# Sliding-window attention with sinks and a squared-ReLU layer on one core: eight sinks per head, and two head pairs to a tile of sinks

## The chip, the cores and the metric

The kernel runs on one core of a Trainium2 chip. The metric is the time of one execution on the device in microseconds (us). The engines are named as in the profile: PE (TensorE, matmuls and transposes), PEld (its weight loads), DVE (VectorE), ACT (ScalarE), POOL (GpSimd) and SP (SyncE, which issues the DMAs).

## The reference, cut to what matters

Attention over 4 batches, 8 heads, 768 positions and a head dimension of 64, in which a query sees the first `n_sink` (4) keys, the sinks, and its own window of the last `window` (128) keys. Then a two-layer network over the 3072 tokens with 512 inputs and 2048 hidden units, with g = s * relu(h)^2 + b between the layers.

```python
keep = is_sink | in_window                    # pos < n_sink, 0 <= rel < window
scores = np.where(keep, scale * q @ k.T, -1e9)
a = np.exp(scores - scores.max(-1, keepdims=True))
a = a / (a.sum(-1, keepdims=True) + 1e-9)
x = (a @ v)                                   # transposed to (B*S, H*D)
r = np.maximum(x @ w_in, 0.0)
out = (s * (r * r) + b) @ w_out
```

## The kernel before

The tokens are cut into 8 chunks of 384 (half a sequence of one batch, in the order `ORDER`), each of 3 blocks of 128 queries. The expert layer of chunk c ("block c" of the run) is interleaved with the attention of chunk c+1, so there are a lone attention chunk at the start, seven mixed blocks, and a lone expert layer at the end. Float32 matmuls run in a rounded form, so an operand is split in a rounded part and its remainder, and two or three matmuls are added.

The expert layer is a list of 32 steps (`moe_steps`): `l1(f)` (12 matmuls of 384 columns, line 598, then ReLU on ACT into the tile `r`, line 601, the square on DVE, line 603, and the split of g on ACT and DVE, lines 605 and 606), and `l2(f)` (9 matmuls of 512 columns, line 617). Their order is l1(0), l1(1), l1(2), l2(0), l1(3), l2(1), ..., l1(15), l2(13), l2(14), l2(15): from step 2 on l1(f) is step 2f - 2, and l2(f) is step 2f + 3. At the last l2 the three output tiles are copied out of PSUM into tiles of the tag `ot` and stored.

Chunks 0 and 1 take another way to attention (`Plain`). Chunks 2 to 7 take `attn_slots`: 24 units (8 heads by 3 query blocks) in a pipeline over slots t. In slot t stand `unit_a` of unit t, `unit_b` of unit t - 4 and `unit_c` of unit t - 7, and at its end the transpose of unit t - 3 (`turn`, line 324).

- `unit_a`: two score matmuls (lines 303 and 304) over the keys of the window and `NS` sinks, 272 columns (144 for the first query block of a sequence), masked minimum on DVE (308), exponential on ACT with the row sums into `zz` (314), addition of the two half windows on POOL (317), and a copy of the sinks' weights, three times, into the tile `psk` of the pair of heads (318).
- `unit_b`: the transposed weights are masked and split into `hl` (337 to 340). After the last unit of a pair 1/sum is made and written, split in two, into columns 96 to 99 of `psk`.
- `unit_c`: the matmuls with the values (368, 376). After the last unit of a head the result goes to the tile `y` (383, 384); after the last of a pair, three 128x128 transposes turn `psk` (390), and the result is copied to `xsk` (392, with a remainder on DVE, 393).
- `sinks` (line 399: one matmul with the sinks' values `vs`, added to y) and `scaled` (line 406: one matmul with the selector `sel`, which spreads 1/sum, multiplied into y), then the split into `k.x`, which the next l1 reads. `load_sinks` fetches `vs` through a staging tile of the tag `ot`.

`ahead` and `ends` in `attn_slots` give the slots of loads, preparation, `sinks` and `scaled` of each pair: loads 2 or 5 slots before the pair's first unit; `sinks` and `scaled` 3 and 4 slots behind the pair's transposes, 2 and 2 for the last pair. Now the transposes of a chunk's four pairs stand in slots 12, 18, 24 and 30.

The loop at lines 771 to 783 gives slots to steps: slot i is issued behind step floor(30 i / 33), so slots 0 and 1, 11 and 12, 22 and 23 share one. This program order is a priority for a planner, which then orders each engine's queue by its own cost model: an instruction that it takes to be ready can go ahead of one that stands before it. TensorE's queue in the trace follows the program order but for a few places.

Tiles of a tag share `bufs` buffers; a tile waits until the tile before it in its buffer has been read for the last time. `psA` has 5 PSUM banks for h, scores, o, ts, os and zb. `r` has 2 buffers (`RB`), `y` 2, `xsk` 1.

Of the kernel before, what the change touches and what calls it, by code (L numbers as in the profile page):

```python
# [6 lines left out]
F32 = mybir.dt.float32  # L7
# [8 lines left out]
P = 128  # L16
B, H, S, D = 4, 8, 768, 64
ORDER = ((0, 0), (1, 0), (0, 1), (1, 1), (2, 0), (2, 1), (3, 0), (3, 1))
NS = 16
BLK = 3  # L20
# [12 lines left out]
NARROW, NEARLY = 2, 8  # L33
RB, VB = 2, 2
E0 = 8
FN, FB, FC = (4, 2), (6, 6), (9, 10)
LB, LC, LD, LDL, L2 = 4, 7, (3, 4), (2, 2), 2


@with_exitstack  # L40
def tile_kernel(ctx, tc, qT, kT, k0, v, vsk, n_sink, window, w, s, b, out):
# [14 lines left out]
    late = []  # L56
    m_all = const.tile([P, 6 * P], MDT, tag="m", name="m_all")
    m_full = [m_all[:, a * P:(a + j + 1) * P] for j, a in ((0, 0), (1, 1), (2, 3))]
# [8 lines left out]
    split = const.tile([P, 2, P], U8, tag="split", name="split")  # L67
    msk = const.tile([P, 3 * W + P + NS], MDT, tag="msk", name="msk")
    m_1, m_odd, m_even = (msk[:, j * W:(j + 1) * W] for j in range(3))
    m_0 = msk[:, 3 * W:]  # L70

# [61 lines left out]
    def constants2():  # L133

        spread = wk.tile([P, P], F32, tag="y", name="spread", bufs=2)
        nc.gpsimd.memset(spread, 0.0)
        for j in range(2):
            nc.gpsimd.affine_select(
                out=spread[96:P].rearrange("p (a d) -> p a d", a=2), in_=spread[96:P].rearrange("p (a d) -> p a d", a=2),
                pattern=[[1, 2], [0, D]], compare_op=ALU.not_equal, fill=1.0, base=2 * j, channel_multiplier=-1)  # L140
# [12 lines left out]
        mask(m_even[:, P:P + NS], snk[:, :NS])  # L153
        cp = nc.gpsimd.tensor_copy
        upm, lom = m_full[2][:, P:2 * P], m_full[2][:, 2 * P:]
        cp(out=m_0[:, NS:], in_=lom)
        for m, l0 in ((m_1, P), (m_even, P + NS), (m_odd, P)):
            cp(out=m[:, :P], in_=upm)
            cp(out=m[:, l0:l0 + P], in_=lom)
        cp(out=m_odd[:, 2 * P:], in_=m_even[:, P:P + NS])  # L160

# [11 lines left out]
    def load_weight(f):  # L173
        if f + 1 < NF:
            raw = place(f + 1).bitcast(I32).rearrange("p c t f -> p c (t f)")
            nc.sync.dma_start(raw, w[f])
            raws[f] = [raw[:, c].rearrange("p (f t) -> p f t", t=2) for c in range(2)]
            if f + 1 < NF - NARROW:
                raws[f] = [raw.rearrange("p c (f t) -> p c f t", t=2)]
        else:  # L180
            raws[f] = []
            for j, tag in enumerate(("vv", "vv", "y", "y")):
                raw = wk.tile([P, DM // 2, 2], I32, tag=tag, name="wraw", bufs=2)
                nc.sync.dma_start(raw.rearrange("p f t -> p (f t)"), w[f, :, j // 2, j % 2 * DM:(j % 2 + 1) * DM])
                raws[f].append(raw)
# [53 lines left out]
    def load_pair(k, pr):  # L239

        pp = Chunk()
        k.pairs[pr] = pp
        half = k.half
        nkb, k0, kw, v0 = 3 + half, (0, 288)[half], (416, 544)[half], half * 2
        pp.q = wk.tile([P, CH], F32, name="qraw", tag="qraw", bufs=1)
        nc.sync.dma_start(pp.q, qT[k.b, pr, :, half * CH:(half + 1) * CH])
        pp.v = wk.tile([P, 4, 2, D], F32, name="vraw", tag="vraw", bufs=1)
        nc.sync.dma_start(pp.v[:, :nkb], v[k.b, pr, :, v0:v0 + nkb])
        for hh in range(2):
            hd = Chunk()  # L250
# [22 lines left out]
    def prep_head(k, h):  # L273
# [18 lines left out]
    def unit_a(k, h, i, sc):  # L292
# [33 lines left out]
    def unit_b(k, h, i, tp):  # L326
# [17 lines left out]
        pp = k.pairs[h // 2]  # L344
        if h % 2 == 1 and i == BLK - 1:
            zr = wk.tile([P, 2, BLK, 2], F32, tag="zr", name="zr")
# [4 lines left out]
            nc.gpsimd.tensor_copy(out=pp.psk[:, :, 96:98], in_=zh.bitcast(F32))  # L351
            nc.vector.tensor_tensor(out=pp.psk[:, :, 98:100], in0=zr[:, 1], in1=zh.bitcast(F32), op=ALU.subtract)

    def unit_c(k, h, i):
# [24 lines left out]
        if i == BLK - 1:  # L379
            a, c = (0, D) if h % 2 == 0 else (D, 0)  # L380
            if h % 2 == 0:
                pp.x = wk.tile([P, CH + P], F32, tag="y", name="y", bufs=2)
            nc.scalar.copy(pp.x[a:a + D], hd.o[c:c + D])
            nc.vector.tensor_tensor(out=pp.x[a:a + D], in0=hd.o[a:a + D], in1=pp.x[a:a + D], op=ALU.add)
            if h % 2 == 1:
                nc.gpsimd.tensor_tensor(out=pp.x[:, CH - P:CH], in0=pp.x[:, CH - P:CH], in1=pp.x[:, CH:], op=ALU.add)
                pp.x = pp.x[:, :CH]
                ts = ps("ts")
                for j in range(BLK):
                    nc.tensor.transpose(ts[:, j * P:(j + 1) * P], pp.psk[:, j, :], ident)  # L390
                pp.xs = wk.tile([P, CH], F32R, tag="xsk", name="xsk", bufs=1)
                nc.scalar.copy(pp.xs, ts[:, :CH])
# [194 lines left out]
    def moe_steps(x, store, wk, before=None, last=False):  # L587
# [3 lines left out]
        def l1(f):  # L591
# [242 lines left out]
```

## Time and profile before

| | |
|---|---|
| median of 3 runs | 736.4 us (736.2 to 736.9) |
| profiled execution, its own time | 739.3 us |
| span of that execution | 737.2 us |
| mean granted clock of TensorE | 0.977 |

An excerpt of the page: the span in 40 equal slices of 18.4 us. Each digit is the busy share of a slice in tenths; PEclk is the clock that TensorE was granted.

```profile
PE   6788899899999999999999999999999999999996
...
DVE  6779999738984788757785588847886589743331
ACT  5978888568774787656884677746775677633222
POOL 2254555348991689616773589816775389710000
PEclk9879989999999999999999999999999999999998
```

A matmul's end is modelled and overlaps the next one's start, so prices of matmuls are read from start to start.

### The profile page before, as it was taken

What the parts mean: (1) busy time and instruction counts of PE and PEld (TensorE: products, weight loads), DVE (VectorE), ACT (ScalarE), POOL (GpSimd) and SP (SyncE); (2) the same over time, 40 slices, a digit from 0 to 9 for tenths busy, and PEclk for the clock granted to TensorE, in tenths of its full rate; (3) what the DMA queues carried; (4) which work ended last, traced back from release to release, by engine and by line L of the source; (5) the groups of instructions that cost most, each with busy time, mean ns of one, the idle gap of its engine ahead of it and who ended that gap; (6) DMA issues with size and microseconds to landing.
All of it is one profiled execution on the core that took longest, in us unless ns stands there. A gap on an engine that the chain in (4) does not pass through costs nothing.

```text
span 737.2 us, 11878 instructions
## 1 busy us (share of the span) xinstructions
PE 704.9 (96%) x3848; PEld 622.0 (84%) x3848; DVE 516.1 (70%) x1213; ACT 480.0 (65%) x1169; POOL 396.3 (54%) x641
## 2 busy tenths in 40 slices
PE   6788899899999999999999999999999999999996
PEld 3367677789988999999998999999999999989895
DVE  6779999738984788757785588847886589743331
ACT  5978888568774787656884677746775677633222
POOL 2254555348991689616773589816775389710000
PEclk9879989999999999999999999999999999999998
DMA  7844122041210212111121222111111212000001
GB/s 280 337 171 193 33 102 72 15 139 51 80 63 31 84 55 65 34 61 54 46 64 44 82 63 64 46 54 49 56 53 45 84 42 59 12 18 26 1 1 47
DMA packets 27221, 53.01 MB, mean 72 GB/s; under 512 B 3472, under 2 KB 15376, under 8 KB 25232
## 3 DMA queue, kind: packets, MB, share of 16 engines
q1 hardware_dynamic: 27152, 52.18, 21.2%
q8 instruction: 32, 0.52, 0.3%
q14 instruction: 37, 0.30, 0.1%
HBM read 45.88 MB, written 6.29 MB: 71 GB/s over the span
## 4 chain that ended last, share of the span: by engine, by line
PE 79%; DVE 10%; DMA 3%; ACT 3%; POOL 2%; issue 1%; SPq 1%; POOLq 0%; ACTq 0%; DVEq 0%
PE po L617 32%; PE h L598 32%; PE o L376 3%; PE sc L303 2%; PE sc L304 2%; PE sc L324 2%; DMA vf<-in_v 2%; DMA w<-in_w 2%; DVE w L214 2%; DVE g L606 1%; DVE wt L213 1%; PE ts L390 1%; POOL w L216 1%; DVE smf L528 1%; DVE r L603 1%
## 5 line engine op out<-in xcount | busy, mean ns | idle before, releaser
L598 PE MATMUL h<-x,w 128*128 128x384 f32 x1536 | 299.8, 344 | 1.1 <-ACT tf L542 0.8
L617 PE MATMUL po<-w,g 128*128 128x512 f32 x1152 | 298.0, 404 | 0.0
L598 PEld LDWEIGHTS h<-x,w 128*128 128x128 f32 x1536 | 268.6, 189 | 6.7 <-ACT tf L542 1.1
L617 PEld LDWEIGHTS po<-w,g 128*128 128x128 f32 x1152 | 212.4, 191 | 45.0 <-issue 2.7
L603 DVE SCALAR_TENSOR_TENSOR r<-h,sb,r 128x384 f32<-128x384 f32 x128 | 78.6, 614 | 82.5 <-ACT r L601 82.2
L606 DVE SCALAR_TENSOR_TENSOR g<-r,sb,g 128x384 fp32r<-128x384 f32 x128 | 102.0, 797 | 39.0 <-ACT g L605 38.2
L340 POOL TENSOR_TENSOR hl<-two,hl 128x256 fp32r<-128x256 f32 x128 | 99.3, 776 | 21.4 <-ACT hl L339 18.2
L601 ACT ACTIVATE r<-h 128x384 f32<-128x384 f32 x128 | 62.3, 487 | 66.7 <-PE h L598 66.5
L605 ACT ACTIVATE g<-r,sb 128x384 fp32r<-128x384 f32 x128 | 78.7, 615 | 34.1 <-DVE r L603 32.8
L317 POOL TENSOR_TENSOR sm<-sm 128x128 f32<-128x128 f32 x128 | 68.0, 531 | 59.5 <-ACT sm L314 55.5
L314 ACT ACTIVATE sm<-sm,negm 128x272 f32<-128x272 f32 (+1 forms) x144 | 73.1, 507 | 35.4 <-DVE negm L308 31.0
L308 DVE CUSTOM_DVE_ANT_0 sm<-sc,msk 128x272 f32<-128x272 f32 (+1 forms) x144 | 60.4, 419 | 40.4 <-PE sc L304 32.6
L284 POOL TENSOR_TENSOR kl<-kraw,kh 128x544 fp32r<-128x544 f32 (+1 forms) x48 | 63.1, 1315 | 21.7 <-ACT kh L282 21.7
L339 ACT CAST hl<-two 128x256 fp32r<-128x256 f32 x128 | 50.6, 395 | 31.6 <-DVE two L337 31.6
L216 POOL TENSOR_TENSOR w<-w 128x1024 int32<-128x1024 int32 (+1 forms) x17 | 32.6, 1919 | 45.6 <-DVE w L214 25.1
L337 DVE TENSOR_TENSOR two<-sc,split 128x256 f32<-128x256 f32 x128 | 53.0, 417 | 4.4 <-POOL hl L340 4.2
L318 POOL COPY psk<-sm 128x48 f32<-128x48 f32 x144 | 40.7, 282 | 26.7 <-ACT sm L314 26.1
L289 POOL TENSOR_TENSOR vv<-vraw,vv 128x256 fp32r<-128x256 f32 (+1 forms) x48 | 34.4, 718 | 24.6 <-ACT vv L288 24.6
L376 PE MATMUL o<-hl,vv 128*128 128x256 f32 (+1 forms) x256 | 44.5, 276 | 0.0
L303 PE MATMUL sc<-kh,qs 128*128 128x272 f32 (+1 forms) x144 | 42.6, 298 | 0.0
L376 PEld LDWEIGHTS o<-hl,vv 128*128 128x128 f32 x256 | 39.6, 189 | 2.9
L304 PE MATMUL sc<-kl,qs 128*128 128x272 f32 (+1 forms) x144 | 41.3, 288 | 0.0
(129 smaller groups left out, 904.4 us busy)
## 6 DMA issues: line engine op xcount, KB each, us to landing
w<-in_w SPq DMA_DIRECT2D x15, 1024.0 KB, 9.0
kraw<-in_kT SPq DMA_DIRECT2D x32, 272.0 KB, 2.6
out<-ot SPq DMA_DIRECT2D x24, 256.0 KB, 2.0
qraw<-in_qT SPq DMA_DIRECT2D x24, 192.0 KB, 2.4
vraw<-in_v SPq DMA_DIRECT2D x16, 256.0 KB, 2.7
kraw<-in_kT SPq DMA_DIRECT2D x16, 208.0 KB, 2.4
vsraw<-in_vsk SPq DMA_DIRECT2D x24, 64.0 KB, 2.0
vraw<-in_v SPq DMA_DIRECT2D x8, 192.0 KB, 2.4
```

Of the source, the lines that this page charges most:

```text
L284: nc.gpsimd.tensor_tensor(out=hd.kl[:, :kw], in0=hd.k[:, :kw], in1=hd.kh[:, :kw].bitcast(F32), op=ALU.subtract)
L308: nc.vector.tensor_tensor_reduce(out=sm[:, :n], in0=sc[:, :n], in1=m, scale=-0.125, scalar=BIG, op0=ALU.add, op1=ALU.min, accum_out=negm[: ...
L314: nc.scalar.activation(sm[:, :n], sm[:, :n], AF.Exp, bias=negm[:, uu], scale=-1.0, accum_out=pp.zz[:, i, hh:hh + 1])
L317: nc.gpsimd.tensor_tensor(out=sm[:, c1:c1 + P], in0=sm[:, p1:p1 + P], in1=sm[:, c1:c1 + P], op=ALU.add)
L340: nc.gpsimd.tensor_tensor(out=lo, in0=both, in1=hi.bitcast(F32), op=ALU.subtract)
L376: nc.tensor.matmul(hd.o[:, q0:q0 + n * P], hd.vv[:, kb, :], hd.hl[:, t, c0 * P:(c0 + n) * P], start=(hd.n == 0), stop=(i == BLK - 1 and kb ...
L598: nc.tensor.matmul(h[:, :CH], weight[f][:, 0, wi, cc * P:(cc + 1) * P], x[xi][:, cc, :], start=(i == 0), stop=(i == 11))
L601: nc.scalar.activation(r, h[:, :CH], AF.Relu, scale=1.0 / WUP)
L603: nc.vector.scalar_tensor_tensor(out=r, in0=h[:, :CH], scalar=sw_ap, in1=r, op0=ALU.mult, op1=ALU.mult)
L605: nc.scalar.activation(gg[:, 0, :], r, AF.Identity, bias=b_ap, scale=1.0)
L606: nc.vector.scalar_tensor_tensor(out=gg[:, 1, :], in0=r, scalar=b_ap, in1=gg[:, 0, :].bitcast(F32), op0=ALU.add, op1=ALU.subtract)
L617: nc.tensor.matmul(po[tb], gg[:, gi, tsl], weight[f][:, 1, wi, :], start=(f == 0 and i == 0), stop=(f == NF - 1 and i == 2))
```

## The change

The number of sinks that the fast way holds per head goes from 16 to 8. Three copies of four heads' sinks then fill 96 rows of a `psk` tile as three copies of two heads' did, and rows 96 to 103 hold 1/sum of two pairs, so two pairs of heads share one `psk` tile, its three transposes and one `xsk`. The transposes stand behind the last unit of every second pair (slots 18 and 30), `sinks` and `scaled` follow 3 and 4, then 6 and 7 slots later, and 2, 2, 3, 3 for the last two pairs; `sel` gets a second half, `load_sinks` moves to 11 slots behind the pair's first unit, and a chunk has 34 slots instead of 33. `y` gets a third buffer and `r` loses one; in block 0 odd f take the buffer of `xsk` for it. One mask moves into another tile. For blocks 1 to 7 a list takes the place of the even spreading: slot t goes behind step t minus the number of entries of `TWOS` not over t, so slots 3/4, 12/13, 15/16, 27/28 and 30/31 share a step, and the last slot, 33, stands behind step 28.

```diff
-NS = 16
+NS = 8
-RB, VB = 2, 2
+RB, VB = 1, 2
+TWOS = (4, 13, 16, 28, 31)
-LB, LC, LD, LDL, L2 = 4, 7, (3, 4), (2, 2), 2
+LB, LC, LD, LDL, L2 = 4, 7, ((3, 4), (6, 7)), ((2, 2), (3, 3)), 2
...
-    m_1, m_odd, m_even = (msk[:, j * W:(j + 1) * W] for j in range(3))
-    m_0 = msk[:, 3 * W:]
+    m_1, m_even = (msk[:, j * W:(j + 1) * W] for j in range(2))
+    m_odd, m_0 = m_all[:, 4 * P:], msk[:, 2 * W:]
...
-    sel = const.tile([P, P], F32R, tag="sel", name="sel")
+    sel = const.tile([P, 2, P], F32R, tag="sel", name="sel")
...
-        for j in range(2):
-            nc.gpsimd.affine_select(
...
+        for j in range(4):
+            row = spread[96:P, j // 2].rearrange("p (a d) -> p a d", a=2)
+            nc.gpsimd.affine_select(out=row, in_=row, pattern=[[1, 2], [0, D]], compare_op=ALU.not_equal, fill=1.0,
+                                    base=2 * j, channel_multiplier=-1)
...
+        mask(m_odd[:, 2 * P:], snk[:, :NS])
...
-        for m, l0 in ((m_1, P), (m_even, P + NS), (m_odd, P)):
+        for m, l0 in ((m_1, P), (m_even, P + NS)):
...
-        cp(out=m_odd[:, 2 * P:], in_=m_even[:, P:P + NS])
...
-        pp.psk = psks[(k.c * (H // 2) + pr) % 2]
+        pp.psk = psks[(k.c * (H // 4) + pr // 2) % 2]
...
-        nc.gpsimd.tensor_copy(out=pp.psk[:, i, :6 * NS].rearrange("p (t x) -> p t x", t=3)[:, :, hh * NS:(hh + 1) * NS],
+        nc.gpsimd.tensor_copy(out=pp.psk[:, i, :12 * NS].rearrange("p (t x) -> p t x", t=3)[:, :, h % 4 * NS:(h % 4 + 1) * NS],
...
+            if h % 4 == 3:
                 ts = ps("ts")
                 for j in range(BLK):
                     nc.tensor.transpose(ts[:, j * P:(j + 1) * P], pp.psk[:, j, :], ident)
-                pp.xs = wk.tile([P, CH], F32R, tag="xsk", name="xsk", bufs=1)
+                pp.xs = k.pairs[h // 2 - 1].xs = wk.tile([P, CH], F32R, tag="xsk", name="xsk", bufs=1)
...
-        nc.tensor.matmul(zb[:, :CH], sel, pp.xs, start=True, stop=True)
+        nc.tensor.matmul(zb[:, :CH], sel[:, pr % 2], pp.xs, start=True, stop=True)
...
-            todo = ((-5, load_pair, pr), (-5, load_keys, h), (-2, load_sinks, pr), (-2, prep_head, h), (-2, load_keys, h + 1),
+            todo = ((-5, load_pair, pr), (-5, load_keys, h), (11, load_sinks, pr), (-2, prep_head, h), (-2, load_keys, h + 1),
...
-            t = 2 * BLK * (pr + 1) - 1 + LC
-            for d, fn in zip(LD if pr < H // 2 - 1 else LDL, (sinks, scaled)):
+            t = 4 * BLK * (pr // 2 + 1) - 1 + LC
+            for d, fn in zip((LD if pr < H // 2 - 2 else LDL)[pr % 2], (sinks, scaled)):
...
-            r = wk.tile([P, CH], F32, tag="r", name="r", bufs=RB)
+            r = wk.tile([P, CH], F32, tag="xsk" if before and f % 2 else "r", name="r", bufs=RB)
...
+    step_of = [t - sum(t >= b for b in TWOS) for t in range(4 * BLK * 2 + LC + LDL[1][1])]
...
-            while i < len(slots) and i * (len(steps) - 2 * (c > 0)) < (j + 1) * len(slots):
+            while i < len(slots) and (step_of[i] <= j if c else i * len(steps) < (j + 1) * len(slots)):
```

## Rows read from the trace of the kernel before

**Rows 1.** The page's first part: each engine's busy us, share of the span, instructions.

```profile
PE 704.9 (96%) x3848; PEld 622.0 (84%) x3848; DVE 516.1 (70%) x1213; ACT 480.0 (65%) x1169; POOL 396.3 (54%) x641
```

**Rows 2.** Stretches: length in us, each engine's busy us, granted clock, DMA share.

```profile
0.00:61.00 61.00, 46.98 (x234) 29.62 (x235) 45.89 (x146) 44.83 (x101) 21.08 (x29) 0.86 0.68 260
61.00:153.00 92.00, 81.25 (x412) 64.57 (x411) 79.49 (x139) 67.46 (x131) 44.39 (x28) 0.93 0.22 77
238.70:324.45 85.75, 85.67 (x486) 78.73 (x485) 63.78 (x149) 59.08 (x151) 59.30 (x103) 1.00 0.19 57
324.45:407.74 83.29, 83.29 (x469) 76.52 (x469) 59.37 (x149) 56.30 (x151) 47.90 (x87) 1.00 0.18 57
```

**Rows 3.** TensorE's waits from 153 to 731 us: total, times, longest.

```profile
PE h L598 <- DVE xsk L393: 0.3, 1, 0.3
```

**Rows 4.** TensorE's waits from 0 to 153 us, the two largest groups.

```profile
PE o L551 <- ACT tf L542: 7.5, 5, 2.4
PE tp L540 <- DVE smf L528: 7.4, 3, 2.9
```

**Rows 5.** Groups by form, TensorE, whole span: the transposes of line 390.

```profile
L390 PE MATMUL ts<-identr,psk 128*128 128x128 f32 x72 | 11.8, 272 | 0.0
```

**Rows 6.** Timeline of TensorE around one triple of L390: start, us, engine, line.

```profile
229.48 0.49 PE L390 MATMUL ts<-identr,psk 128*128 128x128 f32 x3
229.73 2.36 PE L598 MATMUL h<-x,w 128*128 128x384 f32 x12
231.93 0.40 PE L617 MATMUL po<-w,g 128*128 128x512 f32 x1
```

**Rows 7.** Timeline of all engines at a chunk's first slots.

```profile
240.67 0.29 PE L303 MATMUL sc<-kh,qs 128*128 128x272 f32 x1
...
240.87 0.49 ACT L601 ACTIVATE r<-h 128x384 f32<-128x384 f32 x1 [0.20 <-PE h L598]
...
241.17 2.28 PE L598 MATMUL h<-x,w 128*128 128x384 f32 x12
...
243.28 0.28 PE L303 MATMUL sc<-kh,qs 128*128 128x272 f32 x1
```

**Rows 8.** Timeline of TensorE, the score matmuls with 144 columns.

```profile
326.40 0.23 PE L303 MATMUL sc<-kh,qs 128*128 128x144 f32 x1
326.47 0.28 PE L304 MATMUL sc<-kl,qs 128*128 128x144 f32 x1
```

**Rows 9.** Timeline of all engines at a chunk's end, from l1(14) on.

```profile
226.83 0.49 ACT L601 ACTIVATE r<-h 128x384 f32<-128x384 f32 x1 [0.60 <-PE h L598]
...
228.66 0.62 DVE L606 SCALAR_TENSOR_TENSOR g<-r,sb,g 128x384 fp32r<-128x384 f32 x1 [0.69 <-ACT g L605]
...
230.29 0.48 ACT L392 CAST xsk<-ts 128x384 fp32r<-128x384 f32 x1
230.29 0.69 DVE L384 TENSOR_TENSOR y<-o,y 64x512 f32<-64x512 f32 x1 [1.01 <-ACT y L383]
...
231.02 0.55 DVE L393 TENSOR_TENSOR xsk<-ts,xsk 32x384 fp32r<-32x384 f32 x1
```

**Rows 10.** Timeline of all engines, first steps of the last block.

```profile
666.45 0.62 DVE L606 SCALAR_TENSOR_TENSOR g<-r,sb,g 128x384 fp32r<-128x384 f32 x1 [0.68 <-ACT g L605]
666.75 0.49 ACT L601 ACTIVATE r<-h 128x384 f32<-128x384 f32 x1 [0.33 <-PE h L598]
```

**Rows 11.** Timeline of all engines while the constants are made.

```profile
2.98 0.29 POOL L138 TENSOR_SCALAR_AFFINE_SELECT spread<-spread 32x128 f32<-32x128 f32 x1
...
7.38 0.52 POOL L158 COPY msk<-m_all 128x128 bf16<-128x128 bf16 x2 [3.64 <-DVE m_all L101]
...
18.15 0.24 DVE L101 TENSOR_SCALAR msk<-sc 128x16 bf16<-128x16 f32 x2
```

**Rows 12.** Timeline of ACT behind l1(13) of the same block.

```profile
222.87 0.58 ACT L383 COPY y<-o 64x512 f32<-64x512 f32 x1
...
223.66 0.62 ACT L605 ACTIVATE g<-r,sb 128x384 fp32r<-128x384 f32 x1
```

More of the change, by code (lines that the diff above doesn't have):

```diff
@@ L56, in tile_kernel @@
     late = []
-    m_all = const.tile([P, 6 * P], MDT, tag="m", name="m_all")
+    m_all = const.tile([P, 6 * P + NS], MDT, tag="m", name="m_all")
     m_full = [m_all[:, a * P:(a + j + 1) * P] for j, a in ((0, 0), (1, 1), (2, 3))]
@@ L67, in tile_kernel @@
     split = const.tile([P, 2, P], U8, tag="split", name="split")
-    msk = const.tile([P, 3 * W + P + NS], MDT, tag="msk", name="msk")
-    m_1, m_odd, m_even = (msk[:, j * W:(j + 1) * W] for j in range(3))
-    m_0 = msk[:, 3 * W:]
+    msk = const.tile([P, 2 * W + P + NS], MDT, tag="msk", name="msk")
+    m_1, m_even = (msk[:, j * W:(j + 1) * W] for j in range(2))
+    m_odd, m_0 = m_all[:, 4 * P:], msk[:, 2 * W:]
     warm = first.tile([P, 512], mybir.dt.bfloat16, tag="warm", name="warm")
@@ L133, in constants2 @@
     def constants2():
-        spread = wk.tile([P, P], F32, tag="y", name="spread", bufs=2)
+        spread = wk.tile([P, 2, P], F32, tag="y", name="spread", bufs=3)
         nc.gpsimd.memset(spread, 0.0)
-        for j in range(2):
-            nc.gpsimd.affine_select(
-                out=spread[96:P].rearrange("p (a d) -> p a d", a=2), in_=spread[96:P].rearrange("p (a d) -> p a d", a=2),
-                pattern=[[1, 2], [0, D]], compare_op=ALU.not_equal, fill=1.0, base=2 * j, channel_multiplier=-1)
+        for j in range(4):
+            row = spread[96:P, j // 2].rearrange("p (a d) -> p a d", a=2)
+            nc.gpsimd.affine_select(out=row, in_=row, pattern=[[1, 2], [0, D]], compare_op=ALU.not_equal, fill=1.0,
+                                    base=2 * j, channel_multiplier=-1)
         nc.scalar.copy(sel, spread)
@@ L182, in load_weight @@
             for j, tag in enumerate(("vv", "vv", "y", "y")):
-                raw = wk.tile([P, DM // 2, 2], I32, tag=tag, name="wraw", bufs=2)
+                raw = wk.tile([P, DM // 2, 2], I32, tag=tag, name="wraw", bufs=2 if tag == "vv" else 3)
                 nc.sync.dma_start(raw.rearrange("p f t -> p (f t)"), w[f, :, j // 2, j % 2 * DM:(j % 2 + 1) * DM])
@@ L243, in load_pair @@
         half = k.half
-        nkb, k0, kw, v0 = 3 + half, (0, 288)[half], (416, 544)[half], half * 2
+        nkb, k0, kw, v0 = 3 + half, (0, 2 * P + 2 * NS)[half], (3 * P + 2 * NS, 4 * P + 2 * NS)[half], half * 2
         pp.q = wk.tile([P, CH], F32, name="qraw", tag="qraw", bufs=1)
@@ L259, in load_keys @@
         hd = k.heads[h]
-        hd.k = wk.tile([P, 544], F32, tag="kraw", name="kraw", bufs=1)
+        hd.k = wk.tile([P, 4 * P + 2 * NS], F32, tag="kraw", name="kraw", bufs=1)
         nc.sync.dma_start(hd.k[:, :hd.kw], kT[k.b, h, :, hd.k0:hd.k0 + hd.kw])
@@ L279, in prep_head @@
         nc.scalar.copy(hd.qs[hd.half], hd.q)
-        hd.kh = wk.tile([P, 544], F32R, tag="kh", name="kh")
-        hd.kl = wk.tile([P, 544], F32R, tag="kl", name="kl")
+        hd.kh = wk.tile([P, 4 * P + 2 * NS], F32R, tag="kh", name="kh")
+        hd.kl = wk.tile([P, 4 * P + 2 * NS], F32R, tag="kl", name="kl")
         nc.scalar.copy(hd.kh[:, :kw], hd.k[:, :kw])
@@ L298, in unit_a @@
         if k.half == 0:
-            c0, n = ((0, 144), (16, 272), (144, 272))[i]
+            c0, n = ((0, NS + P), (NS, W), (NS + P, W))[i]
         else:
-            c0, n = ((0, 272), (128, 272), (272, 272))[i]
+            c0, n = ((0, W), (P, W), (W, W))[i]
         qs = slice(i * P, (i + 1) * P)
@@ L345, in unit_b @@
         if h % 2 == 1 and i == BLK - 1:
+            z0 = 12 * NS + h // 2 % 2 * 4
             zr = wk.tile([P, 2, BLK, 2], F32, tag="zr", name="zr")
@@ L350, in unit_b @@
             nc.vector.tensor_copy(zh, zr[:, 1])
-            nc.gpsimd.tensor_copy(out=pp.psk[:, :, 96:98], in_=zh.bitcast(F32))
-            nc.vector.tensor_tensor(out=pp.psk[:, :, 98:100], in0=zr[:, 1], in1=zh.bitcast(F32), op=ALU.subtract)
+            nc.gpsimd.tensor_copy(out=pp.psk[:, :, z0:z0 + 2], in_=zh.bitcast(F32))
+            nc.vector.tensor_tensor(out=pp.psk[:, :, z0 + 2:z0 + 4], in0=zr[:, 1], in1=zh.bitcast(F32), op=ALU.subtract)
     def unit_c(k, h, i):
@@ L381, in unit_c @@
             if h % 2 == 0:
-                pp.x = wk.tile([P, CH + P], F32, tag="y", name="y", bufs=2)
+                pp.x = wk.tile([P, CH + P], F32, tag="y", name="y", bufs=3)
             nc.scalar.copy(pp.x[a:a + D], hd.o[c:c + D])
@@ L447, in slot @@
             return f
-        return k, [slot(t) for t in range(n + LC + LDL[1])]
+        return k, [slot(t) for t in range(n + LC + LDL[1][1])]
     class Plain:
@@ L812 @@
     vsk = np.zeros((B, H // 2, P, P), v.dtype)
-    for t in range(3):
-        for hh in range(2):
-            r0 = t * 2 * NS + hh * NS
-            vsk[:, :, r0:r0 + NS, hh * D:(hh + 1) * D] = v[:, hh::2, :NS]
+    for t, pr, hh in np.ndindex(3, H // 2, 2):
+        r0 = (t * 4 + pr % 2 * 2 + hh) * NS
+        vsk[:, pr, r0:r0 + NS, hh * D:(hh + 1) * D] = v[:, 2 * pr + hh, :NS]
     w_in, w_out = np.asarray(inputs["moe_w_in"]), np.asarray(inputs["moe_w_out"])
```

## The prediction

> **What bounds the kernel now.** I read the engines' busy times first: TensorE has a matmul in flight for 704.9 us, no other engine for more than 516.1 us [rows 1]. A busy share is a mean over stages, so the table by stretch came next [rows 2]. Three regimes are to be seen there. Up to 153 us (the first attention chunk, and the first expert block with its weight preparation) TensorE is idle for 14.0 + 10.8 us. From there each expert block that carries an attention chunk is full: 85.67 of 85.75 us, 83.29 of 83.29 us, at a granted clock of 1.00, while ACT, DVE and POOL stand idle for 22 us and more. The last block has no attention. So I asked for TensorE's own waits. From 153 to 731 us the list has one entry, 0.3 us [rows 3]; before 153 us stand its two largest groups of waits, 7.5 and 7.4 us, the longest wait 2.9 us [rows 4]. Hence in the six blocks that this change touches, a TensorE instruction removed is time removed, work taken from or given to the other engines is hidden, and an order of slots can gain nothing: it can only make a new wait.
>
> **The change part by part.** The sum is made against the profiled execution, which took 739.3 us (span 737.2 us and 2.1 us around it); the median of the runs shown is 736.4 us, 2.9 us less, and the difference is carried over to it unchanged.
>
> *Transposes of sinks and 1/sum.* 72 are there now, three for each of 24 pairs [rows 5]; two pairs sharing a tile need 36. Their busy time, 272 ns each, overlaps their neighbours and is no price. What counts is from start to start: the triple begins at 229.48, the twelve L598 matmuls behind it at 229.73, and L617 behind those at 231.93: 2.45 us for both [rows 6]. Twelve L598 matmuls behind a score matmul take 241.17 to 243.28 = 2.11 us [rows 7]. The triple costs 0.34 us; 12 go: 12 x 0.33 to 0.34 = 4.0 us.
>
> *Eight sinks instead of sixteen.* Each of the 144 units has two score matmuls, 8 columns narrower. Four matmuls of 272 columns take 240.67 to 241.17 = 0.125 us each [rows 7]; the first of 144 columns takes 326.40 to 326.47 = 0.07 us [rows 8]. That is (0.125 - 0.07)/128 = 0.43 ns a column, or 0.46 ns by 0.125/272. 288 x 8 x 0.45 ns = 1.0 us.
>
> *The work that goes with them on other engines* (12 copies L392 of 0.48 us on ACT, 12 L393 of 0.55 us on DVE [rows 9], a third copy's width on POOL, shorter keys, exponentials and masks) lies beside a full TensorE [rows 2]: nothing gained. The sinks' and scaling matmuls keep their number and their 384 columns.
>
> *One buffer for r.* In blocks 1 to 7 the ReLU (L601) of f+1 must now wait for L606 of f. In the last block, where L598 groups follow closest, L606 of the first f runs from 666.45 for 0.62 us, to 667.07, and the next L601 started at 666.75 [rows 10]: it will start some 0.35 us later, and the third some 0.7 us later (0.35 + 2.45 - 2.11, by the chain of 2.45 us from L601 to the end of L606 [rows 9] and the 2.11 us of an L598 group [rows 7]). Behind it on ACT stand exponentials and L605; what waits for them on TensorE is l2(f), two steps or over 4 us later, and one of five PSUM banks is held that much longer. I take 0; if this cover failed, six blocks times 0.35 to 0.7 us = 2 to 4 us. In block 0, odd f take the other tag, so two buffers alternate as before.
>
> *Sink loads moved* from 2 slots before their pair to 11 slots behind its start. Each issues one DMA on SP, one ACT copy and one POOL subtraction, the same number as before; they leave the start of a chunk, where SP's loads of keys stood behind them, and in their new place the staging tile was freed several slots earlier. 0, by the idle time of ACT and POOL; no gain either, since TensorE did not wait there.
>
> *Constants.* Two more affine selects (0.29 us each) and a larger memset fall into a POOL idle time of 3.64 us ahead of 7.38; three POOL copies go, and one small DVE mask of 0.12 us comes (0.24 us for two) [rows 11]. 0; without that idle time some 1 us.
>
> *The list of slots.* Steps are, in order, l1(0), l1(1), l1(2), l2(0), l1(3), ... Now slots 0/1, 11/12 and 22/23 share a step; then 3/4, 12/13, 15/16, 27/28, 30/31 will. A transpose keeps at least two steps (over 4 us) behind its scores, as now. The tight place is the chunk's end. Now the triple (slot 30) comes behind l2(12), and l1(15) and l2(13) stand between it and the sinks' matmul (slot 32). Afterwards the triple comes behind l1(14), and l2(12) alone stands between. With S the triple's start, the sinks' matmul is due at S + 0.34 + 2.11 = S + 2.45. In the trace xs was ready at 231.02 + 0.55 = 231.57 = S + 2.09, with ACT and DVE free [rows 6, 9]. New is that the chain of l1(14) runs at the same moment: 226.83 to 228.66 + 0.62 in the trace, 2.45 us [rows 9]. ACT's L601 starts at about S - 0.16 (0.36 us of unit c's three matmuls, 0.2 us from the last L598's successor, as 240.67 to 240.87 [rows 7]). If the copies of y and xs go ahead of L605 on ACT, and their DVE partners ahead of L606, xs comes at S + 2.1 to 2.3: no wait. If all of them queue behind L605, ACT is free at S + 1.64, and L383, L384, L393 follow (0.6 + 0.7 + 0.6): S + 3.55, 1.1 us late. The order is the planner's, and in the same situation, behind l1(13), it put L383 at 222.87 ahead of L605 at 223.66 [rows 12]. I take 0 and keep 1.1 us per chunk as the other end.
>
> *Sum:* 4.0 + 1.0 = 5.0 us: 739.3 to 734.3 us for a profiled execution, 736.4 to **731.4 us** for the median.
>
> Two rules bear on this. The trace says that between 238.70 and 324.45 us the matmuls' row was full and TensorE did not wait [rows 2, 3]. The Trainium skill (Perfetto Trace Analysis, section "Identifying the Most-Contended Engine") says that matmul busy time is a poor measure of nearness to the limit and that LDWEIGHTS busy time is to be used; by that the stretch is at 78.73 of 85.75 us and might swallow what is removed (rival B). Start-to-start times that scale with the columns speak against it, but the rule keeps a small chance. The Trainium skill (TensorE: Matmul & The Clock Gate, section "Back-to-back issue gap") gives N/2.4 + 2.5 ns between matmuls: 56 ns for 128 columns; by that 36 transposes are an estimated 2.0 us and the sum 3.0 us. The trace has 0.11 us for a transpose, twice that; I keep the trace (rival C has the cheaper reading, worked out from rows).
>
> **The rivals.**
> A, the wait at the chunk's end. xs is late for the sinks' matmul in all six chunks: 6 x 1.1 = 6.6 us against 5.0 gained, 738.0 us. For: one step between instead of two, and the ACT and DVE chain of l1(14) alongside. Against: the order seen in [rows 12], and ACT and DVE are a quarter idle. It ends slower by 0.2% from (5.0 + 1.5)/6 = 1.08 us a chunk; a smaller lateness of 0.3 to 0.9 us gives 733 to 736.5.
> B, TensorE's matmuls only look full, and the removed ones fall into slack: 736.4 us. For: 7 us a block without a weight load. Against: [rows 3], and [rows 6 to 8], where time follows columns.
> C, a transpose costs one pass, as a matmul of its width: 0.07 x 128/144 = 0.062 us [rows 8], 36 x 0.062 + 1.0 = 3.2 us: 733.2 us. Against: the triple's 0.34 us.
> D, the first 153 us are ordered anew. The planner sets ACT's and DVE's order there by its own times, and a shifted constant or tile can move one wait of up to 2.9 us in or out [rows 4]: 734.3 or 728.5 us. For: 25 us of idle TensorE with no single cause. Against: nothing in that stretch is changed by over 0.2 us.
>
> **How the numbers follow.** The forecast has 0.62 (its own range 730 to 732.9). A has 0.06 in full and 0.12 in part, B 0.03, C 0.03, D 0.08 to the late side and 0.06 to the early. A measurement of this kernel tells 0.2%, 1.5 us, from no change. Faster (below 734.9): 0.62, two thirds of partial A, C, most of late D and early D: 0.85. Slower (above 737.9): 0.06. The same: 0.09. The range takes in D on both sides and most of partial A, and leaves out A in full and B: 728.6 to 735.1 us.
>
> **What would show it.** L390 has 36 matmuls; score matmuls have 264 and 136 columns. A block with a chunk takes 0.66 + 0.17 = 0.8 us less (85.75 to 84.9, 83.29 to 82.5), TensorE's waits from 153 us on stay under 1 us, and the first 153 us keep their length to about 1 us. L601 starts later only at f = 1 and 2. Waits of L399 for DVE's L393 would show A; unchanged blocks B; blocks shorter by 0.5 us C; another length of the first 153 us D. The forecast is wrong if the blocks' gain is not about 5 us, or if a wait of TensorE not in the trace of before takes it back.

## The result, and the profile after

The changed kernel takes 747.7 us (median of 4, 745.3 to 750.5), the kernel before 736.7 us beside it: 1.014 of it, 95% interval 1.010 to 1.019. The forecast was 731.4 us, faster, with a range of 728.6 to 735.1 us.

Its page, engines and the granted clock:

```profile
PE 703.2 (94%) x3812; PEld 616.3 (83%) x3812; DVE 509.6 (68%) x1202; ACT 474.7 (64%) x1157; POOL 391.1 (52%) x640
...
PEclk8879989999999999999999999999999999999999
```

Its stretches, in the columns of [rows 2]: the time up to the first l1, and two mixed blocks:

```profile
0.00:48.00 48.00, 33.31 (x158) 18.60 (x158) 32.10 (x122) 31.87 (x75) 13.85 (x25) 0.77 0.62 237
243.00:329.80 86.80, 84.79 (x478) 77.19 (x477) 61.99 (x147) 58.10 (x149) 58.10 (x103) 1.00 0.18 55
329.80:414.30 84.50, 83.15 (x466) 75.67 (x465) 58.51 (x147) 55.41 (x150) 47.73 (x87) 1.00 0.19 55
```

TensorE stands idle for 2.01 and 1.35 us in them where it stood for 0.08 and 0 [rows 2]. (These stretches miss the blocks' edges by up to 0.3 us, so the busy times are not set against each other; from first l1 to first l1 TensorE's busy time falls by 0.60 and 0.42 us.) Every one of the six blocks is like that. The first row accounts for another part: the same stretch of the kernel before is

```profile
0.00:45.30 45.30, 31.28 (x159) 16.36 (x159) 32.12 (x121) 31.75 (x75) 13.99 (x26) 0.83 0.66 251
```

2.7 us shorter, at a granted clock of 0.83 instead of 0.77, with the same order of ACT's instructions; it is the start's clock, which varies from run to run (last section). Of the 9.2 us between the two spans, 2.7 are the start, 7.6 the six blocks, and -1.1 the rest.

TensorE's waits from 156 us on (total us, count, longest us), against one of 0.3 us in [rows 3]:

```profile
PE sc L325 <- DVE y L386: 7.7, 6, 1.3
PE o L378 <- DVE two L338: 2.9, 8, 0.5
PE sc L325 <- POOL vv L290: 0.5, 1, 0.5
```

(Lines are 1 to 3 higher than before: L325 was L324, L338 L337, L386 L384, L350 to L354 L348 to L352, L393 L390.) Neither of the first two waits is for what the named instruction makes. The transpose L325 reads `sm`; L386 reads a head's result `o`. The matmul L378 of a head's first result reads `hl`; L338 reads the transposed weights of a later unit out of their bank. What they have in common is `psA`: the transpose needs a free bank of its five, and L386 frees the one that holds `o`. In program order the tiles of `psA` from that `o` on are `o`, scores, `ts`, scores and `h`, and the waiting transpose writes the sixth. So TensorE, whose queue in the trace goes in order, stands until DVE has read a bank. The two places on TensorE in a block:

```profile
274.35 2.35 PE L601 MATMUL h<-x,w 128*128 128x384 f32 x12
277.19 0.65 PE L378 MATMUL o<-hl,vv 128*128 128x256 f32 x4 [0.49 <-DVE two L338]
...
289.96 0.28 PE L305 MATMUL sc<-kl,qs 128*128 128x264 f32 x1
291.51 0.30 PE L325 MATMUL sc<-identr,sm 128*128 128x128 f32 x1 [1.26 <-DVE y L386]
```

L305 to L325 is 1.55 us. This L325 is the transpose of slot 19, one slot behind the triple of the second pair. At the same place of the kernel before, L304 to L324 is 0.13 us; its 1/sum chain runs as early (L348), but L384 has freed its bank at 287.47:

```profile
284.02 1.22 DVE L348 TENSOR_SCALAR zr<-zz 128x6 f32<-128x6 f32 x1
...
286.78 0.69 DVE L384 TENSOR_TENSOR y<-o,y 64x512 f32<-64x512 f32 x1
...
287.59 0.29 PE L304 MATMUL sc<-kl,qs 128*128 128x272 f32 x1
287.72 0.27 PE L324 MATMUL sc<-identr,sm 128*128 128x128 f32 x1
```

And DVE after, ahead of the two waits, without a pause:

```profile
273.60 0.42 DVE L350 TENSOR_SCALAR zr<-zz 128x6 f32<-128x6 f32 x1
274.06 0.19 DVE L351 RECIPROCAL zr<-zr 128x6 f32<-128x6 f32 x1
274.29 0.58 DVE L352 CAST zh<-zr 128x6 fp32r<-128x6 f32 x1
274.90 0.17 DVE L354 TENSOR_TENSOR psk<-zr,zh 128x6 f32<-128x6 f32 x1
275.10 1.13 DVE L284 TENSOR_TENSOR qs<-qraw,qs 64x384 fp32r<-64x384 f32 x1
276.26 0.43 DVE L309 CUSTOM_DVE_ANT_0 sm<-sc,m_all 128x264 f32<-128x264 f32 x1
...
276.62 0.42 DVE L338 TENSOR_TENSOR two<-sc,split 128x256 f32<-128x256 f32 x1
...
288.60 0.71 DVE L609 SCALAR_TENSOR_TENSOR g<-r,sb,g 128x384 fp32r<-128x384 f32 x1
289.22 0.17 DVE L350 TENSOR_SCALAR zr<-zz 128x6 f32<-128x6 f32 x1
...
290.12 0.17 DVE L354 TENSOR_TENSOR psk<-zr,zh 128x6 f32<-128x6 f32 x1
290.20 0.43 DVE L309 CUSTOM_DVE_ANT_0 sm<-sc,m_all 128x264 f32<-128x264 f32 x1
...
290.67 0.69 DVE L386 TENSOR_TENSOR y<-o,y 64x512 f32<-64x512 f32 x1
```

L350 to L354 make 1/sum of a pair. In the program they stand in `unit_b` of the pair's last unit, four slots behind its exponential; the planner takes them early: in the trace they start 0.6 to 1.6 us behind the exponential's start, 11 to 30 us before the triple that reads their result, and take 1 to 1.5 us ahead of the score minimum (L309) and of L338 or L386, which frees the bank.

### The profile page after: what moved, and what is told of

It reads as the page before. It is cut to its first block, busy times and chain, and to the rows that moved or that the text cites. A ratio compares the mean times of both kernels' runs of the same rounds, so it can differ in the third digit from the quotient of the medians.

```text
span 746.4 us, 11859 instructions
## 1 busy us (share of the span) xinstructions
PE 703.2 (94%) x3812; PEld 616.3 (83%) x3812; DVE 509.6 (68%) x1202; ACT 474.7 (64%) x1157; POOL 391.1 (52%) x640
## 4 chain that ended last, share of the span: by engine, by line
PE 70%; DVE 16%; ACT 6%; POOL 3%; issue 3%; DMA 1%; SPq 0%; ACTq 0%; POOLq 0%; DVEq 0%
PE po L620 29%; PE h L601 28%; DVE g L609 3%; PE o L378 3%; PE sc L325 2%; DVE sm L309 2%; PE sc L304 2%; PE sc L305 2%; PE tp L543 1%; DVE qs L284 1%; DVE wt L214 1%; PE o L554 1%; DVE y L386 1%; ACT r L604 1%; DVE w L215 1%
## 5 line engine op out<-in xcount | busy, mean ns | idle before, releaser
L606 DVE SCALAR_TENSOR_TENSOR r<-h,sb,r 128x384 f32<-128x384 f32 x128 | 78.9, 616 | 107.5 <-ACT r L604 106.5
L609 DVE SCALAR_TENSOR_TENSOR g<-r,sb,g 128x384 fp32r<-128x384 f32 x128 | 102.8, 804 | 35.6 <-ACT g L608 33.9
L341 POOL TENSOR_TENSOR hl<-two,hl 128x256 fp32r<-128x256 f32 x128 | 99.1, 776 | 11.3 <-ACT hl L340 10.4
L315 ACT ACTIVATE sm<-sm,negm 128x264 f32<-128x264 f32 (+1 forms) x144 | 71.9, 499 | 50.9 <-DVE negm L309 49.2
L285 POOL TENSOR_TENSOR kl<-kraw,kh 128x528 fp32r<-128x528 f32 (+1 forms) x48 | 59.9, 1249 | 29.4 <-ACT kh L283 29.2
L338 DVE TENSOR_TENSOR two<-sc,split 128x256 f32<-128x256 f32 x128 | 53.1, 417 | 0.2
L319 POOL COPY psk<-sm 128x24 f32<-128x24 f32 x144 | 35.9, 250 | 25.3 <-ACT sm L315 25.2
L325 PE MATMUL sc<-identr,sm 128*128 128x128 f32 x144 | 39.8, 276 | 8.3 <-DVE y L386 7.7
L378 PE MATMUL o<-hl,vv 128*128 128x256 f32 (+1 forms) x256 | 44.6, 276 | 3.0 <-DVE two L338 2.9
L378 PEld LDWEIGHTS o<-hl,vv 128*128 128x128 f32 x256 | 39.3, 188 | 9.1 <-issue 5.9
L309 DVE CUSTOM_DVE_ANT_0 sm<-sc,m_all 128x264 f32<-128x264 f32 x64 | 27.2, 425 | 25.2 <-PE sc L305 21.1
L284 DVE TENSOR_TENSOR qs<-qraw,qs 64x384 fp32r<-64x384 f32 x48 | 41.6, 867 | 3.7 <-ACT qs L280 2.6
L304 PE MATMUL sc<-kh,qs 128*128 128x264 f32 (+1 forms) x144 | 43.1, 300 | 0.0
```

The costliest lines, as they stand in the source:

```text
L285: nc.gpsimd.tensor_tensor(out=hd.kl[:, :kw], in0=hd.k[:, :kw], in1=hd.kh[:, :kw].bitcast(F32), op=ALU.subtract)
L304: nc.tensor.matmul(sc[:, :n], hd.qs[:, qs], hd.kh[:, c0:c0 + n], start=True, stop=False)
L315: nc.scalar.activation(sm[:, :n], sm[:, :n], AF.Exp, bias=negm[:, uu], scale=-1.0, accum_out=pp.zz[:, i, hh:hh + 1])
L341: nc.gpsimd.tensor_tensor(out=lo, in0=both, in1=hi.bitcast(F32), op=ALU.subtract)
L378: nc.tensor.matmul(hd.o[:, q0:q0 + n * P], hd.vv[:, kb, :], hd.hl[:, t, c0 * P:(c0 + n) * P], start=(hd.n == 0), stop=(i == BLK - 1 and kb ...
L606: nc.vector.scalar_tensor_tensor(out=r, in0=h[:, :CH], scalar=sw_ap, in1=r, op0=ALU.mult, op1=ALU.mult)
```

## The experiments

Block times below are from the first l1 of a block to the next one's, for a block of the second and of the first half-sequence: 85.7 and 83.3 us before, 87.1 and 84.2 us after. Ratios are to the kernel before, run on the same chip; a run without a ratio was executed once and is read by its blocks. Single waits named in the text are from start to start, some 0.16 us more than the idle time in the fences: 0.64, 0.42 and 1.42 us after, for 0.49, 0.26 and 1.26.

**The list or the buffer of r.** Theory L: the list of slots is the cause. Theory R: the single buffer of `r`.

The list taken out of the changed kernel:

```diff
-            while i < len(slots) and (step_of[i] <= j if c else i * len(steps) < (j + 1) * len(slots)):
+            while i < len(slots) and i * (len(steps) - 2 * (c > 0)) < (j + 1) * len(slots):
```

> The changed kernel with the even spreading of slots in place of the list, all else as changed. Theory L (the list crowds five slots into the steps 11 to 13, DVE falls behind, and TensorE waits for PSUM banks): TensorE's idle time per mixed block falls from 2.0 us to about 0.2, blocks of 84.9 and 82.5 us, 736.6 - 5 = 731 to 734 us (the first 50 us vary with the granted clock). Theory R (one buffer of r delays the ReLU, holds h's PSUM bank longer and starves the scores): nothing changes but places, blocks stay near 86.7 and 84.5, 743 to 748 us.

0.996 (0.993 to 0.998), 735.7 us, blocks 85.1 and 83.1 us: most of what L had, its 731 to 734 us not reached. The waits shrink to these, over all blocks:

```profile
PE h L601 <- DVE r L606: 0.9, 3, 0.3
PE sc L325 <- DVE y L403: 0.5, 1, 0.5
PE o L378 <- DVE y L386: 0.4, 1, 0.4
PE h L601 <- DVE two L338: 0.2, 1, 0.2
```

The list alone, on the kernel before (the condition above the other way round):

```diff
+    step_of = [t - sum(t >= b for b in (4, 13, 16, 28, 31)) for t in range(24 + LC + LDL[1])]
```

> The kernel before with the list of slots alone. Theory L: 1.9 us of new waits in each of six blocks and no gain beside them: blocks of 87.6 and 85.2 us, 736.6 + 11 = 745 to 750 us. Theory R: 736 to 738 us.

1.022 (1.017 to 1.027), 755.8 us, blocks 89.0 and 85.3 us, worse than L had it:

```profile
PE h L598 <- DVE y L384: 9.6, 6, 1.8
PE sc L324 <- DVE two L337: 4.6, 4, 1.2
```

Even l1's matmuls wait for a bank here. The buffer of `r` alone, on the kernel before:

```diff
-RB, VB = 2, 2
+RB, VB = 1, 2
-            r = wk.tile([P, CH], F32, tag="r", name="r", bufs=RB)
+            r = wk.tile([P, CH], F32, tag="xsk" if before and f % 2 else "r", name="r", bufs=RB)
```

> The kernel before with one buffer of r (odd f of the first mixed block in the buffer of xsk). Theory L: blocks as before, 85.75 and 83.29 us, 736 to 738 us. Theory R: about 1.9 us more in each block, 745 to 750 us.

1.0005 (0.998 to 1.003), blocks 85.76 and 83.27 us: R falls. The fourth kernel undid both, and paid for the buffers with earlier sinks:

```diff
-RB, VB = 1, 2
+RB, VB = 2, 2
-LB, LC, LD, LDL, L2 = 4, 7, ((3, 4), (6, 7)), ((2, 2), (3, 3)), 2
+LB, LC, LD, LDL, L2 = 4, 7, ((2, 2), (3, 3)), ((2, 2), (3, 3)), 2
...
-                pp.x = wk.tile([P, CH + P], F32, tag="y", name="y", bufs=3)
+                pp.x = wk.tile([P, CH + P], F32, tag="y", name="y", bufs=2)
...
```

> The changed kernel with the even spreading, two buffers of r again, and two of y instead of three, for which sinks and scaled of the first two pairs stand 2, 2, 3, 3 slots behind the transposes. Theory L: as the run with the even spreading alone, 731 to 734 us. Theory R: this one alone reaches 731 to 734 us, the even spreading alone does not. If both edits matter it is the fastest of the four by over 1 us.

Neither: 1.011 (1.006 to 1.015), blocks 86.3 us, and 88.7 and 87.2 us in the first half-sequences. `sinks` and `scaled` of two pairs, four banks and four DVE instructions that read them, now fall into two slots close behind the triple, and waits of the same kind come back without the list. That this placing makes them is likely, since they stand in slots 20 and 21, but it was not tested by itself:

```profile
PE sc L325 <- DVE y L386: 4.6, 4, 2.0
PE h L601 <- DVE two L338: 4.3, 6, 0.9
PE sc L325 <- DVE two L338: 2.8, 3, 1.2
```

**Which entries of the list.** The changed kernel with other lists. First without 15/16 sharing a step, then without 12/13.

```diff
-TWOS = (4, 13, 16, 28, 31)
+TWOS = (4, 13, 22, 28, 31)
```

> The changed kernel, its list with slots 21/22 sharing a step instead of 15/16. Theory X (two shared steps three slots apart overload DVE, which then frees PSUM banks late): the waits of 0.64, 0.42 and 1.42 us in a mixed block of the second half-sequence shrink to under 0.5 us together, blocks 85.2 and 82.8 us, against 87.07 and 84.23. Theory Y (any shared step that holds a head's preparation, as 12/13 does, is too much): the wait behind 12/13 stays, 0.6 us, and the later ones go: 85.7 and 83 us.

87.4 and 83.1 us: the wait behind 12/13 stays (0.66 us), and three others of 0.4 to 1.1 us come from slot 19 on, where 21/22 meets the first pairs' sinks; the first half-sequences get better. X falls for the first wait, Y for the rest.

```diff
-TWOS = (4, 13, 16, 28, 31)
+TWOS = (4, 7, 16, 28, 31)
```

> The changed kernel, its list with slots 6/7 sharing a step instead of 12/13. Theory X: the waits of TensorE shrink to under 0.5 us a block, 85.2 and 82.8 us. Theory Y: 6/7 and 15/16 hold a head's preparation too and each costs 0.4 to 1.4 us: blocks stay at 86 to 87 us and 84 us.

85.1 and 82.6 us, with the wait behind the triple's slot left at 0.3 to 1.1 us. Y falls: 6/7 and 15/16 hold a preparation and cost little. Timed:

> The kernel with slots 6/7 sharing a step instead of 12/13, timed: blocks of 85.1 and 82.6 us as in the look, six blocks 2 to 4 us below the kernel before, 0.995 of it. If the start's varying clock decides instead, 1.000 with an interval of 0.3%.

0.997 (0.996 to 0.999): less than the 0.995 expected, but clear of 1.000. Its blocks are 85.4 and 82.6 us.

```diff
-TWOS = (4, 13, 16, 28, 31)
+TWOS = (8, 14, 29, 31)
```

> The changed kernel with another list: slots 7/8, 13/14, 28/29 and 30/31 share a step, so that none of them holds the taking down of a head's result, and the last two stand in the chunk's emptying pipeline; the last slot is behind step 29 as in the even spreading. Theory X and D: waits of TensorE under 0.3 us a block, 84.9 and 82.5 us, the fastest of all, 731 to 733 us where the kernel before takes 736.6. Theory Y: 13/14 holds a preparation and costs 0.5 us a block, as the even spreading's 0.2 to 0.7 us: no faster than that.

1.002 (0.999 to 1.004), blocks 85.6 to 86.9 and 83.0 us: a wait behind 13/14, of 0.8 to 1.3 us in three blocks of a second half-sequence and of 1.9 us in the fourth. My rule for placing the shared steps was wrong.

```diff
-TWOS = (4, 13, 16, 28, 31)
+TWOS = (1, 5, 9, 28, 31)
```

> The changed kernel with a list in which slots 0/1, 4/5, 8/9, 27/28 and 30/31 share a step: the sharing stands where the pipeline fills or empties, no two within three slots of each other in its full part. Theory D (a slot costs TensorE nothing as long as DVE keeps up): waits under 0.3 us a block, 84.9 and 82.5 us, 736.6 - 5 = 731.5 us, 0.993 of the kernel before. Rival: 4/5 and 8/9 hold a head's preparation or its end, and cost as 12/13 did, 0.6 us each: 86 and 83.7 us, 738 us.

0.998 (0.996 to 1.000), blocks 85.8 and 82.5 us: right for the first half-sequences; in the others the wait behind the triple's slot stays (0.86 us), and one of 0.39 us is added. The slots' positions alone don't explain the waits.

**DVE's load.** A plain copy in place of one DVE instruction, the list as in the changed kernel:

```diff
-        nc.vector.tensor_tensor(out=hd.qs[other], in0=hd.q, in1=hd.qs[hd.half].bitcast(F32), op=ALU.subtract)
+        nc.vector.tensor_copy(hd.qs[other], hd.q)
```

> The changed kernel with its list; the remainder of q (L284) is not computed, a plain copy of q stands in its place on DVE, which takes about 0.3 us where the subtraction took 0.6 to 1.1. This leaves out a part of the computation. Theory D (DVE's lateness is what keeps the PSUM banks): the waits in a block fall from 2.5 to under 1 us, blocks of 85.5 and 83 us. Theory P (the order of TensorE's queue asks for results sooner than the chain of engines can give them, whatever DVE has to do): 87 and 84.2 us as before.

85.65 and 83.6 us: the waits behind 12/13 and 15/16 are gone. TensorE's queue in the blocks is the same, instruction for instruction, so P falls for them: the same order can be met. One wait remains, 1.2 us behind the triple's slot:

```profile
PE sc L325 <- DVE y L386: 6.1, 6, 1.4
```

But the edit is no clean test of DVE's load. By its median the copy is no faster than the subtraction, where 0.3 us was expected (min, median and max in ns; the changed kernel first):

```profile
L284 DVE TENSOR_TENSOR qs<-qraw,qs x48: 552/784/1583, 139.7 to 630.3; 64x384 fp32r<-64x384 f32 x48
L284 DVE CAST qs<-qraw x48: 353/786/1443, 135.8 to 618.1; 64x384 fp32r<-64x384 f32 x48
```

DVE's busy time falls by 1.1 us in a block of the second half-sequence, and its order changes too: the copy does not read ACT's half of `qs`, and in place of the L284 that ran between the 1/sum chain and L309 at 275.10 above, it runs ahead of the chain. Which of the two removes the waits is not shown.

The triple moved out of slot 18 (into a function of its own, called at the end of slot 19):

```diff
...
-        ends = {}
+        ends = {4 * BLK - 1 + LC + 1: [(turn_sinks, 1)]}
```

> The changed kernel with its list; the triple of transposes behind the second pair stands in slot 19 instead of 18, behind the next scores, so that its PSUM bank is asked for after the bank of the head's result has been read. Theory B (the wait of 1.4 us before a transpose of weights in slot 18 is for a PSUM bank: the triple took the fifth one): that wait falls under 0.5 us, blocks 86 and 82.9 us. Theory D (DVE is late in reading the head's result in any case): it stays or moves one slot on, blocks 87 and 84.2 us as before.

86.7 and 84.0 us: the wait stays at the same transpose, that of slot 19 (the text above takes it for slot 18), shrinks to 1.03 us and has another releaser. B as stated falls, since more than 0.5 us stays. But the triple still takes a bank of `psA` ahead of this transpose, so the run does not show that its bank has no part:

```profile
PE sc L325 <- DVE two L338: 5.9, 6, 1.1
PE o L378 <- DVE two L338: 2.9, 8, 0.5
```

The same with the list `(4, 7, 9, 28, 31)`:

> The changed kernel with slots 3/4, 6/7, 8/9, 27/28 and 30/31 sharing a step, and the second pair's triple in slot 19. Theories B and D: no waits over 0.3 us, 84.9 and 82.5 us, 0.993 of the kernel before. Rival: three shared steps within six slots overload DVE as 12/13 with 15/16 did: 86 to 87 us.

1.005 (1.003 to 1.008), blocks 86 and 83.4 us. With the crowding at the start comes a new wait, `PE o L370 <- POOL hl L341`, 0.9 to 1.0 us in each block.

**The 1/sum chain.** Theory D1: the chain's early place is the cause. The edit holds its first instruction in program order on DVE; list, buffers and everything else stay as changed.

```diff
-            nc.vector.tensor_scalar(out=zr[:, 0], in0=pp.zz, scalar1=1e-9, scalar2=None, op0=ALU.add)
+            tc.keep_in_program_order(nc.vector.tensor_scalar(out=zr[:, 0], in0=pp.zz, scalar1=1e-9, scalar2=None, op0=ALU.add))
```

> The changed kernel with its list; the first instruction of the 1/sum chain (L350) is held in its place in program order on DVE, so that the chain no longer runs several slots early. Theory D1 (the early chain of about 1 us ahead of the score minimum and of L386 makes the third wait): the wait of 1.42 us in slot 18 or 19 falls under 0.5 us, blocks 86.1 and 83 us against 87.07 and 84.23. Theory D2 (the third wait is the ordinary work of the slots): 86.8 to 87 and 84 us.

84.7 and 82.2 us: all three waits are gone, not only the third, while TensorE's queue in the blocks has the same order, instruction for instruction, as in the changed kernel. TensorE's waits of the whole run from 153 us on, and the same two blocks:

```profile
PE sc L325 <- DVE y L386: 0.2, 1, 0.2
```

```profile
236.10:320.80 84.70, 84.55 (x480) 77.62 (x479) 60.85 (x147) 58.21 (x150) 58.05 (x103) 1.00 0.19 57
320.80:403.00 82.20, 82.20 (x464) 75.48 (x463) 58.16 (x147) 55.40 (x150) 47.19 (x87) 1.00 0.20 57
```

DVE at the place of the third wait, to be set beside 288.60 to 290.67 above. L609 is followed by the score minimum at once:

```profile
280.53 0.71 DVE L609 SCALAR_TENSOR_TENSOR g<-r,sb,g 128x384 fp32r<-128x384 f32 x1
281.17 0.42 DVE L309 CUSTOM_DVE_ANT_0 sm<-sc,m_all 128x264 f32<-128x264 f32 x1
...
281.63 0.69 DVE L386 TENSOR_TENSOR y<-o,y 64x512 f32<-64x512 f32 x1
```

and on TensorE L305 to L325 is 0.43 us instead of 1.55 (0.13 in the kernel before):

```profile
282.04 0.28 PE L305 MATMUL sc<-kl,qs 128*128 128x264 f32 x1
282.47 0.30 PE L325 MATMUL sc<-identr,sm 128*128 128x128 f32 x1
```

Timed:

> The changed kernel with its own list and the 1/sum chain held in program order, timed. By the look: blocks of 84.7 and 82.2 us, 8 us below the kernel before on the same chip, 0.989 with an interval of 0.3%. It is as good as the even spreading with the same line (0.9889) or the other list (0.9897), so the list is then worth nothing and costs nothing.

0.990 (0.988 to 0.993). With the plain copy added:

> The same with the remainder of q replaced by a plain copy, which leaves out a part of the computation. Theories D and D1 together: no wait of over 0.3 us is left in a mixed block, 84.9 and 82.5 us, although the list is unchanged. If 1 us or more of waits stays, DVE's load is not the whole cause.

84.4 and 82.2 us and no wait at all: it adds 0.3 us in one kind of block, so nothing else of size is left. With the even spreading, and with the list `(4, 7, 16, 28, 31)`:

> The even spreading with the 1/sum chain held in program order. Theory D1: its remaining waits of 0.2 to 0.7 us a block go, 84.9 and 82.5 us; 0.994 of the kernel before. Theory D2: as the even spreading alone, 85.07 and 83.13 us, 0.996.

> The list with slots 6/7 sharing a step instead of 12/13, and the 1/sum chain held in program order. Theory D1: the wait of 0.3 to 0.9 us a block that was left goes, 84.9 and 82.5 us, 0.994 to 0.995 of the kernel before. Theory D2: as that list alone, 85.1 to 85.4 and 82.6 us, 0.997.

0.989 (0.985 to 0.992), blocks 84.4 and 82.5 us, and 0.990 (0.986 to 0.993), blocks 84.5 and 82.2 us. More than the 0.994 that D1 had for both, and the three spreadings are then equal within their intervals. The control, the line alone on the kernel before:

> The kernel before with the 1/sum chain held in program order, nothing else. Theory D1 in its narrow form (the early chain hurts only where slots are crowded): TensorE had 0.1 us of waits a block there, so 85.7 and 83.3 us as before, 1.000 of the kernel before. If the chain costs the kernel before too, blocks are shorter by up to 0.5 us, 0.996.

1.002 (1.000 to 1.004), blocks 85.6 and 83.85 us: no gain there, and a small loss.

## Why the prediction was wrong

**What bounds the kernel** was right: in the six blocks what decides is TensorE's work plus its waits.

**The removed work** was right in kind and set too low. With the chain held the six blocks take 503.7 us against 510.2 before, 6.5 us less, where the sum has 5.0; a block without waits is 1.1 us (83.3 to 82.2) to 1.3 us (85.7 to 84.4) shorter, against 0.84 us. Added up from start to start in a block of the second half-sequence (before, and the list `(4, 7, 16, 28, 31)` with the chain held), two triples take 0.57 us with themselves and 0.23 us with the l1 matmuls, 0.80 in place of 0.66 to 0.68; the scores fall by 0.27 us in place of 0.17; another 0.2 us falls on the matmuls with the values and 0.1 us on the scaling ones, for which the sum has nothing and which no run explains.

**The step that failed is the list of slots.** I took 0 for it, because a transpose keeps two steps behind its scores and because only the chunk's end looked tight. The two steps count TensorE's time. What had to be asked is whether DVE gets through two slots' work before TensorE wants the next bank. With slots 12/13 and 15/16 sharing steps, and the chain of 1/sum of the pair just finished taken early, it doesn't: blocks are 2.4 us longer in the second half-sequences and 2.0 us in the others than with the same list and the chain held. The list is needed for most of this (0.996 without it, 1.022 with it alone), and so is the chain's place (0.990 with the list and the chain held). The row that bore on it stood in the prediction, ACT, DVE and POOL idle for 22 us a block [rows 2]; I read it as a cover for anything that goes to those engines. It is a mean over 85 us, and a wait of 1.3 us is made in a stretch of some 5 us (286.11 to 291.36) in which DVE doesn't pause.

**Rival A** had the right kind of cause, the planner's order on DVE against a step of TensorE taken out, but at the chunk's end, where nothing happened: no wait for L396 or of the sinks' matmul is in the changed kernel's list. In [rows 12] I took one case in which the planner put a useful instruction ahead as a sign that it does so in general. It also puts ahead what nobody waits for.

**D**, the start, came true in size for 2.7 us, but that is luck: it came by the granted clock and not by a new order. **The single buffer of r** was right at 0 by its own run. The moved sink loads and the constants had none; no wait of TensorE in the blocks or new order at the start speaks against their 0. B and C fell when the waits were gone: blocks 1.1 us and more shorter are neither 0 nor the 0.5 us of C.

What stays open: holding L350 in order rearranges DVE's queue behind it too, so it is shown that the waits hang on this instruction's place, not that its own 1 us is the whole of each of them, and no run held another instruction instead. That the waits are for banks rests on the releasers in the trace and on the count of tiles in the program; no run gave `psA` another bank. Either edit alone, the even spreading or the held chain, brings the kernel below the one before; together they gain no more than the second.

## What to carry to other kernels

Where one engine is full, a new order has no cover in the others' mean idle time: look, in the few microseconds where work is brought together, at the engine that frees the full engine's buffers, and at what stands in its queue ahead of the freeing instruction. If a planner orders the queues, an instruction with few inputs that nobody needs soon may be taken early, as here; holding one such instruction in its place was worth some 14 us in the six blocks here (517.8 to 503.7 us; the ratio to the kernel before went from 1.014 to 0.990), more than the work that the change removes. A wait named after an instruction that makes none of the waiter's data can be a wait for a buffer: look for what both use.

## What the runs showed of the hardware

The time of one and the same kernel varies by up to 9 us: on one chip 17 executions of the kernel before took from 736.0 us at a mean granted clock of 0.984 to 744.9 us at 0.969, where the prediction reckoned that a measurement tells 1.5 us. The traces show part of this in the first 50 us, where TensorE often stands and is granted one or the other of its two levels: with the same order of ACT's and TensorE's instructions, the first l1 starts at 44.0 us with a granted clock of 0.93 (the run with the list `(4, 7, 9, 28, 31)`) and at 48.1 us with 0.77 (the one with `(8, 14, 29, 31)`). It hides a gain of 0.5% from few runs. The blocks of the trace, at a granted clock of 1.00, do not have it: they mostly repeat to 0.1 us within a trace, and to 0.3 us between two traces of one kernel.

The same DVE subtraction of 64x384 elements (L284 after) takes from 552 to 1583 ns, with a median of 784. The Trainium skill (SBUF — State Buffer, section "Who interferes with whom") says that a DVE instruction with two SBUF inputs contends with a POOL instruction that reads SBUF. The trace agrees: L609, which has two such inputs, takes 0.60 to 0.78 us where POOL is busy for less than half of it, and 0.61 to 2.78 us, with a median of 0.94, elsewhere, while L606, L338 and L386, which read PSUM, never take more than 0.62, 0.43 and 0.70 us. Two SBUF inputs are not the whole of it, since the plain copy of L284 has one and took from 353 to 1443 ns, and no run here took POOL's instructions away.
